# Packed keys for the second batch of a fused attention and gated feed-forward kernel, and weight units stored before their split

## The chip, the core and the metric

The kernel runs on one core of a Trainium2 chip. The metric is device time in microseconds (us), the median of several runs. On the core TensorE (PE in the profile) multiplies matrices, VectorE (DVE), ScalarE (ACT) and GpSimd (POOL) work element by element, and SyncE (SP) issues most transfers (DMA). Sums of TensorE go to PSUM, which has eight banks; an evacuation is the copy of a sum out of PSUM.

## The reference

Softcapped attention over 4 batches of 12 heads, 448 positions and 64 columns a head; its result, 1792 tokens of 768 columns, goes through a gated feed-forward layer.

```python
def _attn_ref(q, k, v, cap):
    scores = np.matmul(q, k.transpose(0, 1, 3, 2)) / np.sqrt(q.shape[-1])
    scores = cap * np.tanh(scores / cap)
    attn = np.exp(scores - np.max(scores, axis=-1, keepdims=True))
    attn = attn / (np.sum(attn, axis=-1, keepdims=True) + 1e-09)
    return np.matmul(attn, v).astype(np.float32)

x = attn_out.transpose(0, 2, 1, 3).reshape(B * S, H * D)
gate = 1.0 / (1.0 + np.exp(-(x @ w_gate)))     # x 1792x768, w_gate and w_val 768x1536
out = (gate * (x @ w_val)) @ w_out             # w_out 1536x768
```

The three weights arrive as 64-bit floats.

## The kernel before

**Precision.** Most products take each factor as two 32-bit parts of reduced precision, `hi` and `lo` (`_Ops.hi`, L207, a rounding copy; `_Ops.lo`, L213, the difference), and add three products. Products of probabilities and values are made in plain fp32 for the first twelve head pairs instead (`direct(n)`, n < 12); such a product shows as two matmul records a piece.

**Attention** (`_bounded_attention`) works on 24 pairs of heads, n = 0 to 23, six a batch. For each pair it transposes keys and queries (`emit_T`, tile `tp`), copies them out as hi and lo (tile `T`), makes scores in four groups of keys (`emit_S`, tile `sc`, a two-bank PSUM tile, head 0 in one bank and head 1 in the other; each matmul uses half of the rows of TensorE, "64*112" in its row), takes tanh out of PSUM into `t` (L392), takes exp once a head (`emit_exp`, L400), and multiplies with the values (`emit_PV`, tile `pv`). The values carry 64 columns of ones, so that `pv` holds the sums of exp too. `emit_rd` copies `pv` out (L479 the sums, L481 the values), a reciprocal and a product follow (L506, `emit_out`). For n < 6 (`packed`) keys stand in three groups of 128 and a last one that holds the last 64 keys of both heads: its scores are three matmuls over all rows (L379), its part of `pv` two fp32 matmuls with half the rows (`emit_R`, L434), and the other part three fp32 matmuls a head (L441). For n = 6 to 11 (`even`) keys stand in four groups of 112: 24 score matmuls (L389) and four fp32 matmuls a head (L450), issued two at a time, each head in the one bank of the pool `ps_v` after the other.

**Feed-forward** (`moe(b)`) takes 36 weight units a batch: 24 units of 18 matmuls into `h` (L836; gate unit, then value unit) and 12 units of 18 into `o` (L927). In batch 0 each unit u is loaded as 64-bit words, converted to fp32 in one of two raw slots of `pair0` (L728 on ACT, L729 to L731 on DVE, five units ahead of its use), split into `wspl` (L207 on ACT, L213 on DVE, three units ahead; four slots, `WB`), and the split unit, 768 KB, is stored to DRAM (L777, tile `wd`) to be loaded again in batches 1 to 3 (L787). Units 0 to 3 are split early and stored through ACT's queue (`next_w`).

**Order.** The attention of batch b+1 is woven into the feed-forward of batch b. `_emit` draws from both generators: a `yield` says how much work was issued, and attention goes on when `done_a * tot_m <= done_m * tot_a`, where `tot_m` is 545 and `tot_a` is 12 times `o.head(b + 1)`. PE and ACT run in exactly this order. DVE, POOL and SP are ordered by a list scheduler.

Of the kernel before, what the change touches and what calls it, by code (L numbers as in the profile page):

```python
# [98 lines left out]
def _load_inside(engines, t, src, n, runs=False):  # L99

    s = _pair(src, n)
    order = "(p c) d -> p c d" if runs else "(c p) d -> p c d"
    for h in range(2):
        engines[h % len(engines)].dma_start(
            out=t[0:src.shape[2] // NCH, :, h, :], in_=s[h].rearrange(order, c=NCH)
        )


def _load_evenly(nc, t, src, n):

    s = _pair(src, n)
    for h in range(2):
        nc.sync.dma_start(
            out=t[0:src.shape[2] // NCH, h * NCH:(h + 1) * NCH],
            in_=s[h].rearrange("(p c) d -> p c d", c=NCH),
        )
# [132 lines left out]
def _bounded_attention(o, x_done):  # L249
# [66 lines left out]
    def load_v(n):  # L316
# [8 lines left out]
        if packed(n):  # L325
            _load_v_packed(nc, s[:, :, 0:D], o.v, n)
        else:
            _load_evenly(nc, s[:, :, 0:D], o.v, n)
# [11 lines left out]
    def emit_T(n):  # L340
# [5 lines left out]
        if even(n):  # L346
            o.transpose_evenly(ps[:, 0, :], t[:, 1])
        else:
            for m in range(NC):
                nc.tensor.transpose(  # L350
                    ps[:, 0, m * P:(m + 1) * P], t[:, 1, m].rearrange("p h d -> p (h d)"), ident
                )
# [2 lines left out]
        w = S if even(n) else BANK
        hi, lo = T[n][:, 0, :, 0:w], T[n][:, 1, :, 0:w]
        if even(n):
            parts = [(hi, lo, ps[:, :, 0:w])]
        else:
            parts = [tuple(  # L360
                x.rearrange("p i s -> p (i s)")[:, 0:BANK + S] for x in (hi, lo, ps)
            )]
        for a, b, x in parts:
            o.hi("a", a, x)
            with o.tc.high_priority(offset=2 * AHEAD_OF):
                o.lo("v", b, x, a)
# [656 lines left out]
```

## Time and profile before

| | us |
| --- | --- |
| median of 3 runs (lowest to highest) | 760.43 (759.23 to 761.16) |
| profiled execution | 758.98 |
| its span on the core | 757.2 |
| PE busy | 742.8 (98%) |
| DVE busy | 467.4 (62%) |
| ACT busy | 349.4 (46%) |
| POOL busy | 202.3 (27%) |

The mean granted clock of TensorE was 0.999 of full speed. The core moved 170.63 MB; the transfers that SP issued took 69.8% of the time of the 16 DMA engines. Busy time says how long an engine had something to run; a row with a bracket names the idle time just before it and what ended that.

### The profile page before, as it was taken

How to read it: one execution, taken by the hardware profiler on the slowest of the kernel's cores; microseconds unless marked ns; L12 is line 12 of the kernel's file. 1: busy time of each engine (PE TensorE's matmuls, PEld its weight loads, DVE VectorE, ACT ScalarE, POOL GpSimd, SP SyncE). 2: the span in 40 equal slices, each digit the busy share in tenths (PEclk: the TensorE clock that was granted, in tenths of full speed). 3: DMA queues.
4: the chain of work that ended last, by engine and by line, in shares of the span. 5: the costliest groups of instructions: out<-in, count | busy, mean ns of one | idle time of the engine just before them, and what ended most of it. 6: DMA issues, size and time to landing. Idle time of an engine off the chain costs nothing.

```text
span 757.2 us, 10267 instructions
## 1 busy us (share of the span) xinstructions
PE 742.8 (98%) x3922; PEld 642.5 (85%) x3922; DVE 467.4 (62%) x503; ACT 349.4 (46%) x383; POOL 202.3 (27%) x223
## 2 busy tenths in 40 slices
PE   8999999999999999999999999999999999999997
PEld 7555878777778888988899988888889999999996
DVE  2698789979998938878786628878785011111000
ACT  5888577667576445555554245555540000000000
POOL 1354000021210516363535306353551000000000
PEclk9999999999999999999999999999999999999999
DMA  4867899999999866555677956644589866665541
GB/s 100 222 161 156 284 346 360 330 307 302 285 267 376 298 212 196 179 186 178 183 222 232 288 185 193 199 143 158 166 234 313 273 223 226 226 225 180 176 168 56
DMA packets 133509, 170.63 MB, mean 225 GB/s; under 512 B 86860, under 2 KB 111948, under 8 KB 133452
## 3 DMA queue, kind: packets, MB, share of 16 engines
q1 hardware_dynamic: 131788, 166.44, 69.8%
q10 hardware_dynamic: 1664, 3.46, 1.3%
q8 instruction: 33, 0.54, 0.3%
q14 instruction: 24, 0.20, 0.1%
HBM read 132.91 MB, written 36.18 MB: 223 GB/s over the span
## 4 chain that ended last, share of the span: by engine, by line
PE 78%; DVE 10%; DMA 3%; SPq 2%; issue 2%; POOL 2%; ACT 2%; DVEq 0%; POOLq 0%; ACTq 0%
PE h L836 43%; PE o L927 18%; PE sc L389 5%; PE pv L450 4%; DVE rd L506 2%; PE pv L459 2%; PE pv L460 2%; DVE pl L213 1%; PE tp L242 1%; DMA v<-in_v_dram 1%; PE pv L441 1%; DVE pair L731 1%; PE tp L350 1%; DVE pair L730 1%; DVE wspl L213 1%
## 5 line engine op out<-in xcount | busy, mean ns | idle before, releaser
L836 PE MATMUL h<-xspl,wspl 128*128 128x448 f32 x1728 | 377.4, 372 | 0.3 <-DVE osb L949 0.3
L836 PEld LDWEIGHTS h<-xspl,wspl 128*128 128x128 f32 x1728 | 321.3, 188 | 42.4 <-issue 15.5
L927 PE MATMUL o<-wspl,gspl 128*128 128x384 f32 x864 | 159.3, 338 | 0.2 <-DVE osb L949 0.2
L927 PEld LDWEIGHTS o<-wspl,gspl 128*128 128x128 f32 x864 | 150.5, 188 | 4.8 <-issue 3.8
L392 ACT ACTIVATE t<-sc,scale 128x896 f32<-128x896 f32 (+1 forms) x90 | 85.9, 1002 | 43.9 <-PE sc L389 43.7
L205 POOL TENSOR_SCALAR gspl<-gate 128x448 fp32r<-128x448 f32 x48 | 35.9, 748 | 251.7 <-DVE gate L880 251.7
L877 ACT ACTIVATE gate<-h 128x448 f32<-128x448 f32 x48 | 26.0, 541 | 161.3 <-PE h L836 159.8
L400 ACT ACTIVATE t<-t,capv 128x1792 f32<-128x1792 f32 (+2 forms) x48 | 83.2, 1738 | 0.1
L880 DVE SCALAR_TENSOR_TENSOR gate<-gate,h 128x448 f32<-128x448 f32 x48 | 29.7, 618 | 77.1 <-PE h L836 72.1
L506 DVE RECIPROCAL rd<-rd 128x448 f32<-128x448 f32 x24 | 70.7, 2946 | 5.3 <-ACT rd L479 3.1
L389 PE MATMUL sc<-T 64*128 64x448 f32 (+1 forms) x540 | 69.1, 382 | 1.9 <-DVE T L213 1.7
L389 PEld LDWEIGHTS sc<-T 64*128 64x128 f32 (+1 forms) x540 | 46.4, 181 | 22.3 <-issue 10.9
L949 DVE TENSOR_SCALAR osb<-o 128x384 f32<-128x384 f32 x22 | 12.0, 553 | 73.1 <-PE o L927 73.0
L412 POOL TENSOR_TENSOR a<-t 128x448 f32<-128x448 f32 x24 | 31.6, 1315 | 84.8 <-ACT t L400 46.9
L213 DVE TENSOR_TENSOR gspl<-gate,gspl 128x448 fp32r<-128x448 f32 x48 | 36.6, 763 | 22.3 <-POOL gspl L205 22.1
L207 ACT ACTIVATE ph<-t 128x1792 fp32r<-128x1792 f32 x24 | 40.7, 1696 | 16.4 <-PE pv L461 10.1
L213 DVE TENSOR_TENSOR pl<-t,ph 128x1344 fp32r<-128x1344 f32 x24 | 45.6, 1899 | 2.4 <-ACT ph L207 1.9
L213 DVE TENSOR_TENSOR T<-tp,T 128x960 fp32r<-128x960 f32 (+1 forms) x24 | 27.3, 1136 | 27.8 <-ACT T L207 27.8
L731 DVE SCALAR_TENSOR_TENSOR pair<-w,pair 128x768 uint16<-128x768 uint32 x36 | 41.7, 1162 | 0.3
L728 ACT ACTIVATE pair<-w 128x768 f32<-128x768 f32 x36 | 32.5, 904 | 18.9 <-DVE wspl L213 7.2
L450 PE MATMUL pv<-t,vo 112*128 112x448 f32 x96 | 40.1, 539 | 0.4 <-ACT t L400 0.4
L730 DVE SCALAR_TENSOR_TENSOR pair<-w,pair 128x768 int32<-128x768 int32 x36 | 35.5, 990 | 0.6
(81 smaller groups left out, 716.3 us busy)
## 6 DMA issues: line engine op xcount, KB each, us to landing
wspl<-wd SPq DMA_DIRECT2D x108, 768.0 KB, 4.4
wd<-wspl SPq DMA_DIRECT2D x32, 768.0 KB, 6.3
w<-in_moe_w_gate_dram SPq DMA_DIRECT2D x12, 768.0 KB, 6.7
w<-in_moe_w_val_dram SPq DMA_DIRECT2D x12, 768.0 KB, 7.0
w<-in_moe_w_out_dram SPq DMA_DIRECT2D x12, 768.0 KB, 7.1
qk<-in_q_dram SPq DMA_DIRECT2D x46, 112.0 KB, 4.1
out_dram<-osb SPq DMA_DIRECT2D x24, 192.0 KB, 3.3
qk<-in_k_dram SPq DMA_DIRECT2D x34, 96.0 KB, 2.7
```

Of the source, the lines that this page charges most:

```text
L205: self.nc.gpsimd.tensor_scalar(dst, src, 1.0, 1.0, ALU.mult, ALU.mult)
L207: self.nc.scalar.activation(dst, src, AF.Copy)
L213: e.tensor_sub(dst, src, hi.bitcast(F32))
L389: nc.tensor.matmul(ps[0:w, j, 0:S], a[rows], r[rows], start=(i == 0), stop=(i == len(ops) - 1))
L392: nc.scalar.activation(Pt[n][0:w, :, m, :], ps[0:w, :, 0:S], AF.Tanh, scale=c["scale"][0:w])
L400: nc.scalar.activation(t, t, AF.Exp, scale=c["cap"][rows])
L450: nc.tensor.matmul(pv, vs[n][0:QC, j * NC + m, :], Pt[n][0:QC, j, m, :], start=(m == 0), stop=(m == NC - 1),)
L506: nc.vector.reciprocal(rd, rd)
L730: nc.vector.scalar_tensor_tensor(xi, top, -2 ** 31, xi, ALU.bitwise_and, ALU.bitwise_or)
L731: nc.vector.scalar_tensor_tensor(half, low.bitcast(U32), 2.0 ** -29, half, ALU.mult, ALU.add)
L836: nc.tensor.matmul(ps, a, r, start=(kk == 0 and i == 0), stop=(kk == KD - 1 and i == 2))
L927: nc.tensor.matmul(ps, a, r, start=(y + kk == 0 and i == 0), stop=(y + kk == KF - 1 and i == 2),)
```

## The change

Three things change. First, `packed` becomes `direct`, so pairs 6 to 11 use the packed form of pairs 0 to 5. For these pairs (`together(n)`) both heads' `pv` stand in one two-bank tile from the pool of the scores, and the last score group of pairs 7 to 11 stands in the bank of `ps_v` that is free by it. The main loop has a new branch for the step after such a pair: the two half-row matmuls, the first score group, both heads' products, four copies out of `pv`, the other three score groups, the transposes, both exps. Second, `o.head` is 23.5 where it was 25, and 17.8 for the last batch; at n = 24 two yields of 5 are added. Third, odd units 5 to 27 (`whole`) are stored once converted, before their split, 384 KB each (tile `wr`), loaded again to a raw slot seven units ahead in batches 1 to 3, and split again there: 12 more splits a batch on ACT and DVE, no split store for these units.

```diff
-    packed = alone
+    packed = direct
+    def together(n):
+        return direct(n) and not alone(n)
...
-    o.head = lambda b: 25 if direct(b * o.NPAIR) else 18.5
+    o.head = lambda b: 23.5 if direct(b * o.NPAIR) else 17.8 if b == B - 1 else 18.5
...
+        if packed(n) and m == NF:
+            if together(n) and n > o.NPAIR:
+                ps = o.ps_v.tile([P, S], F32, tag="v", name=f"sc{n}_{m}")
+            else:
+                ps = o.two_banks(f"sc{n}_{m}")[:, 0, 0:S]
+            for i, (a, r) in enumerate(ops):
+                nc.tensor.matmul(ps, a, r, start=(i == 0), stop=(i == len(ops) - 1))
+            nc.scalar.activation(Pt[n][:, 0, NF, :], ps, AF.Tanh, scale=c["scale"])
+            return 4
...
+    two = {}
     def new_pv(n, j):
-        if alone(n) and not (j == 1 and n % 2 == 0):
+        if together(n):
+            if j == 0:
+                two[n] = o.two_banks(f"pv{n}")
+            pv = two[n][:, j, 0:S] if j == 0 else two.pop(n)[:, j, 0:S]
+        elif alone(n) and not (j == 1 and n % 2 == 0):
...
+        if n > 0 and together(n - 1):
+            emit_R(n - 1)
+            emit_S(n, 0)
+            yield 5
+            for j in range(2):
+                for _ in emit_PV(n - 1, j):
+                    yield 6
+            for j in range(2):
+                emit_rd(n - 1, j)
+            emit_out(n - 1)
+            vs.pop(n - 1)
+            load_v(n + 1)
+            yield 5
+            emit_S(n, 1)
+            emit_S(n, 2)
+            if not packed(n):
+                yield 8
+            emit_S(n, NF)
+            yield 8
+            emit_T(n + 1)
+            qks[n + 2] = o.load_qk(n + 2, packed(n + 2))
+            yield 5
+            if n % o.NPAIR == 0:
+                yield None
+            emit_exp(n, 0)
+            if not direct(n):
+                emit_P(n, 0)
+            emit_exp(n, 1)
+            split_v(n + 1)
+            if direct(n):
+                yield 15
+            continue
...
+        if not live:
+            yield 5
...
+        if not live:
+            yield 5
...
+    WHOLE = 28
...
+    def whole(u):
+        u %= NU
+        return u % 2 == 1 and KEEP <= u < WHOLE and o.early == KEEP
...
         w_raw[u] = x
+        if whole(u):
+            d = dram.tile([P, UN], F32, name=f"wr{u}")
+            w_dram[u] = d
+            nc.sync.dma_start(out=d, in_=x)
...
-        if not u < KEEP:
+        if KEEP <= u < NU and not whole(u):
             store_w(u, s)
...
+    def load_raw_to(n):
+        while loaded["raw"] < min(n, B * NU):
+            u = loaded["raw"]
+            loaded["raw"] += 1
+            if NU <= u and whole(u):
+                at = loaded["slot"] % WRAW * UN
+                loaded["slot"] += 1
+                x = c["pair0"][:, at:at + UN]
+                nc.sync.dma_start(out=x, in_=w_dram[u % NU])
+                w_raw[u] = x
...
-            if KEEP <= u < o.early or NU <= u:
+            if KEEP <= u < o.early or NU <= u and not whole(u):
...
         load_to(u + WB)
+        load_raw_to(u + LEAD + 2)
```

In the rows that follow a tile has its name and numbers (`pv6`, `h0_0_1` is batch, which, chunk; `wspl5` the split unit 5), and lines of the changed kernel have moved: L836 is L865 there, L927 is L956, L434 L413, L441 L420, L389 L365, L728 L741, L207 L197, L479 and L481 are L449 and L451.

PE where batch 0's feed-forward begins, before: the third unit's matmuls, the scores of pair 7, then the first products of pair 6 with its values.

```order
L836 MATMUL h0_0_1_812<-xspl0_4_655,wspl2_521 128x448 x3
L389 MATMUL sc7_0_835<-T7_725 112x448 x6
L389 MATMUL sc7_1_843<-T7_725 112x448 x6
L836 MATMUL h0_0_1_812<-xspl0_5_697,wspl2_521 128x448 x3
L836 MATMUL h0_1_1_868<-xspl0_0_319,wspl3_603 128x448 x3
L836 MATMUL h0_1_1_868<-xspl0_1_405,wspl3_603 128x448 x3
L836 MATMUL h0_1_1_868<-xspl0_2_491,wspl3_603 128x448 x3
L836 MATMUL h0_1_1_868<-xspl0_3_573,wspl3_603 128x448 x3
L450 MATMUL pv6_0_881<-t6_663,vo6_658 128x448 x2
```

The same place on PE after: the half-row products of pair 6 are the first instruction after the third unit.

```order
L865 MATMUL h0_0_1_822<-xspl0_4_663,wspl2_521 128x448 x3
L865 MATMUL h0_0_1_822<-xspl0_5_706,wspl2_521 128x448 x3
L413 MATMUL pv6_848<-t6_672,vo6_666 128x448 x2
L365 MATMUL sc7_0_852<-T7_731 128x448 x6
L865 MATMUL h0_1_1_876<-xspl0_0_319,wspl3_607 128x448 x3
L865 MATMUL h0_1_1_876<-xspl0_1_405,wspl3_607 128x448 x3
```

The products of pair 6 now stand after 54 matmuls of `h`, ahead of the scores of pair 7; they stood after 66 and 12 score matmuls of pair 7.

ACT around the end of unit 18 of batch 0, before: the gate of `h0_0_9`, the conversion of unit 23, the split of unit 22, the copies out of pair 9's first head, the tanh of pair 10's later score groups.

```order
L877 ACTIVATE gate0_9_1568<-h0_0_9_1580 128x448
L728 ACTIVATE pair0_66<-w64_23_1477 128x768
L207 ACTIVATE wspl22_1608<-pair0_66 128x768
L479 ACTIVATE rd9_1620<-pv9_0_1562 64x448
L481 ACTIVATE xraw1_928<-pv9_0_1562 64x448
L392 ACTIVATE t10_1533<-sc10_2_1623,scale_94 112x2x448
L392 ACTIVATE t10_1533<-sc10_3_1631,scale_94 112x2x448
```

The same place on ACT after:

```order
L906 ACTIVATE gate0_9_1579<-h0_0_9_1589 128x448
L741 ACTIVATE pair0_66<-w64_23_1502 128x768
L197 ACTIVATE wspl22_1620<-pair0_66 128x768
L449 ACTIVATE rd9_1632<-pv9_1555 64x448
L451 ACTIVATE xraw1_929<-pv9_1555 64x448
L449 ACTIVATE rd9_1632<-pv9_1555 64x448
L451 ACTIVATE xraw1_929<-pv9_1555 64x448
L368 ACTIVATE t10_1558<-sc10_1_1650,scale_94 128x2x448
L368 ACTIVATE t10_1558<-sc10_2_1658,scale_94 128x2x448
```

All four copies of pair 9 stand in a row behind gate, conversion and split, and ahead of the tanh of pair 10's second score group.

PE after, around it: from the last products of pair 9 to the scores of pair 10 that take the bank pair of `pv9` again.

```order
L420 MATMUL pv9_1555<-t9_1321,vo9_1172 128x448 x3
L865 MATMUL h0_0_9_1589<-xspl0_4_663,wspl18_1449 128x448 x3
L865 MATMUL h0_0_9_1589<-xspl0_5_706,wspl18_1449 128x448 x3
L865 MATMUL h0_1_9_1625<-xspl0_0_319,wspl19_1504 128x448 x3
L865 MATMUL h0_1_9_1625<-xspl0_1_405,wspl19_1504 128x448 x3
L865 MATMUL h0_1_9_1625<-xspl0_2_491,wspl19_1504 128x448 x3
L865 MATMUL h0_1_9_1625<-xspl0_3_577,wspl19_1504 128x448 x3
L365 MATMUL sc10_1_1650<-T10_1476 128x448 x6
L365 MATMUL sc10_2_1658<-T10_1476 128x448 x6
L358 MATMUL sc10_3_1666<-T10_1476 128x448 x3
```

Between the last product of pair 9 and group 2 of pair 10 stand 18 matmuls of `h` and one score group.

PE at the end of attention, in the feed-forward of batch 2, before: from the last product of pair 23's first head to the first of its second head.

```order
L461 MATMUL pv23_0_5053<-ph23_0_4992,vs23_4831 128x448
L927 MATMUL o2_0_2_4982<-wspl97_4897,gspl2_3903 128x384 x6
L927 MATMUL o2_0_0_4980<-wspl98_4951,gspl2_3903 128x384 x6
L927 MATMUL o2_0_1_4981<-wspl98_4951,gspl2_3903 128x384 x6
L459 MATMUL pv23_1_5097<-pl23_1_5085,vs23_4831 128x448
```

The same place on PE after:

```order
L431 MATMUL pv23_0_5147<-ph23_0_5066,vs23_4894 128x448
L956 MATMUL o2_0_2_5035<-wspl99_5036,gspl2_3934 128x384 x6
L956 MATMUL o2_0_0_5033<-wspl100_5057,gspl2_3934 128x384 x6
L956 MATMUL o2_0_1_5034<-wspl100_5057,gspl2_3934 128x384 x6
L956 MATMUL o2_0_2_5035<-wspl100_5057,gspl2_3934 128x384 x6
L956 MATMUL o2_0_0_5033<-wspl101_5099,gspl2_3934 128x384 x6
L956 MATMUL o2_0_1_5034<-wspl101_5099,gspl2_3934 128x384 x6
L429 MATMUL pv23_1_5211<-pl23_1_5179,vs23_4894 128x448
```

The second head of pair 23 stands 36 matmuls of `o` behind the first, where 18 stood. Ahead of the first head there are 24 between it and the row sums of pair 22 (`dn22`), where there were 6.

## Rows read from the trace of the kernel before

**Rows 1.** The page: busy time, share of the span and instructions of each engine.
```profile
PE 742.8 (98%) x3922; PEld 642.5 (85%) x3922; DVE 467.4 (62%) x503; ACT 349.4 (46%) x383; POOL 202.3 (27%) x223
```

**Rows 2.** Chain of waits: start us, length us, engine, output tile, line, count.
```profile
113.47 1.41 PE sc L389 x12
...
117.50 1.51 PE pv L450 x4
119.00 2.44 PE h L836 x12
...
570.40 3.12 PE o L927 x18
```

**Rows 3.** Timeline of PE, 24 to 36: start, length, line, tile, shape, count [idle before].
```profile
26.61 0.92 PE L434 MATMUL pv<-t,vo 64*128 64x448 f32 x4
27.46 2.52 PE L441 MATMUL pv<-t,vo 128*128 128x448 f32 x6
...
32.20 2.43 PE L441 MATMUL pv<-t,vo 128*128 128x448 f32 x6
34.56 0.47 PE L389 MATMUL sc<-T 64*128 64x448 f32 x2
```

**Rows 4.** Timeline of PE, 535 to 605, the end of attention.
```profile
562.40 0.44 PE L459 MATMUL pv<-pl,vs 128*128 128x448 f32 x1 [0.99 <-DVE xraw L488]
...
568.69 0.47 PE L459 MATMUL pv<-pl,vs 128*128 128x448 f32 x1 [1.48 <-DVE pl L213]
```

**Rows 5.** Timeline of PE: start of batch 0's feed-forward, and tile tp of pair 12.
```profile
73.71 0.99 PE L242 MATMUL tp<-ident,qk 112*128 112x112 f32 x8 [0.49 <-ACT t L392]
74.47 10.58 PE L836 MATMUL h<-xspl,wspl 128*128 128x448 f32 x51
...
90.14 1.77 PE L450 MATMUL pv<-t,vo 112*128 112x448 f32 x4 [0.44 <-ACT t L400]
...
214.57 0.66 PE L350 MATMUL tp<-ident,qk 128*128 128x128 f32 x4 [0.90 <-ACT t L392]
```

**Rows 6.** Timeline of ACT, 60 to 92.
```profile
87.56 0.85 ACT L207 ACTIVATE wspl<-pair 128x768 fp32r<-128x768 f32 x1 [2.72 <-PE h L836]
...
88.31 3.45 ACT L400 ACTIVATE t<-t,capv 112x1792 f32<-112x1792 f32 x2
```

**Rows 7.** Chain of waits, 80 to 92: the store of split unit 1.
```profile
82.07 5.41 DMA wd<-wspl
```

**Rows 8.** Timeline of ACT, 130 to 200: gate, conversion of unit 23, copies of pair 9.
```profile
179.69 0.55 ACT L877 ACTIVATE gate<-h 128x448 f32<-128x448 f32 x1 [3.41 <-PE h L836]
180.13 0.90 ACT L728 ACTIVATE pair<-w 128x768 f32<-128x768 f32 x1
...
182.34 0.54 ACT L481 ACTIVATE xraw<-pv 64x448 f32<-64x448 f32 x1
```

**Rows 9.** Timeline of ACT, 100 to 130: the conversion of unit 11.
```profile
111.97 0.91 ACT L728 ACTIVATE pair<-w 128x768 f32<-128x768 f32 x1
```

**Rows 10.** Timeline of DVE: last conversion step of units 9 and 21.
```profile
107.97 1.06 DVE L731 SCALAR_TENSOR_TENSOR pair<-w,pair 128x768 uint16<-128x768 uint32 x1
...
174.32 1.01 DVE L731 SCALAR_TENSOR_TENSOR pair<-w,pair 128x768 uint16<-128x768 uint32 x1
```

**Rows 11.** Stores of split units (768 KB) from issue to landing, 100 to 200.
```profile
DMA to landing us min/median/max: 3.6/6.2/8.3
```

**Rows 12.** The page's DMA issues: KB each, us to landing.
```profile
out_dram<-osb SPq DMA_DIRECT2D x24, 192.0 KB, 3.3
```

**Rows 13.** Timeline of PE: first and warm 128x128 matmuls, and the last matmuls.
```profile
1.64 3.78 PE L72 MATMUL warm<-ident 128*128 128x128 f32 x16 [1.64 <-POOL ident masks.py:199]
...
13.80 1.96 PE L304 MATMUL fill<-ident 128*128 128x128 f32 x16
...
745.22 6.40 PE L927 MATMUL o<-wspl,rest 128*128 128x384 f32 x36
```

**Rows 14.** Windows after the last matmul: length, engines' busy time, granted clock.
```profile
756.20:756.40 0.20, 0.00 (x0) 0.00 (x0) 0.00 (x0) 0.00 (x0) 0.00 (x0) 0.87 0.00 0
```

More of the change, by code (lines that the diff above doesn't have):

```diff
@@ L96, in _pair, with _load_inside @@
     return src[b, 2 * p:2 * p + 2]
-def _load_inside(engines, t, src, n, runs=False):
+def _load_inside(engines, t, src, n):
     s = _pair(src, n)
-    order = "(p c) d -> p c d" if runs else "(c p) d -> p c d"
     for h in range(2):
         engines[h % len(engines)].dma_start(
[L105 to L115, printed above, removed]
+            out=t[0:src.shape[2] // NCH, :, h, :],
+            in_=s[h].rearrange("(c p) d -> p c d", c=NCH),
         )
@@ L324, in load_v @@
         nc.gpsimd.memset(s[:, :, D:], 1.0)
[L325 to L328, printed above, removed]
+        _load_v_packed(nc, s[:, :, 0:D], o.v, n)
         vs[n] = s
@@ L345, in emit_T @@
         ps = o.two_banks(f"tp{n}")
[L346 to L352, printed above, removed]
+        for m in range(NC):
+            nc.tensor.transpose(
+                ps[:, 0, m * P:(m + 1) * P], t[:, 1, m].rearrange("p h d -> p (h d)"), ident
+            )
         o.transpose_evenly(ps[:, 1, :], t[:, 0])
         T[n] = ap.tile([P, 2, 2, BANK], F32R, tag="T", bufs=1, name=f"T{n}")
[L355 to L366, printed above, removed]
+        a, b, x = (
+            y.rearrange("p i s -> p (i s)")[:, 0:BANK + S]
+            for y in (T[n][:, 0], T[n][:, 1], ps)
+        )
+        o.hi("a", a, x)
+        with o.tc.high_priority(offset=2 * AHEAD_OF):
+            o.lo("v", b, x, a)
     def emit_S(n, m):
@@ L371, in emit_S @@
             Pt[n] = ap.tile([P, 2, NC, S], F32, tag="t", bufs=2, name=f"t{n}")
-        w = QC if even(n) else P
-        kh, kl = (T[n][:, i, 0, m * w:(m + 1) * w] for i in range(2))
+        kh, kl = (T[n][:, i, 0, m * P:(m + 1) * P] for i in range(2))
         qh, ql = (T[n][:, i, 1, 0:S] for i in range(2))
         ops = ((kh, qh), (kl, qh), (kh, ql))
-        ps = o.two_banks(f"sc{n}_{m}")
-        if packed(n) and m == NF:
-            for i, (a, r) in enumerate(ops):
-                nc.tensor.matmul(
-                    ps[:, 0, 0:S], a, r, start=(i == 0), stop=(i == len(ops) - 1)
-                )
-            nc.scalar.activation(
-                Pt[n][:, 0, NF, :], ps[:, 0, 0:S], AF.Tanh, scale=c["scale"]
-            )
-            return 4
+        if packed(n) and m == NF:
[7 more added lines that the diff above has]
+            return 4
+        ps = o.two_banks(f"sc{n}_{m}")
         for i, (a, r) in enumerate(ops):
@@ L389, in emit_S @@
                 nc.tensor.matmul(
-                    ps[0:w, j, 0:S], a[rows], r[rows], start=(i == 0), stop=(i == len(ops) - 1)
+                    ps[:, j, 0:S], a[rows], r[rows], start=(i == 0), stop=(i == len(ops) - 1)
                 )
-        nc.scalar.activation(
-            Pt[n][0:w, :, m, :], ps[0:w, :, 0:S], AF.Tanh, scale=c["scale"][0:w]
-        )
+        nc.scalar.activation(Pt[n][:, :, m, :], ps[:, :, 0:S], AF.Tanh, scale=c["scale"])
         return 4
     def emit_exp(n, j):
-        rows = slice(0, QC if even(n) else P)
-        t = Pt[n][rows, j, 0:NF if packed(n) and j == 1 else NC]
-        nc.scalar.activation(t, t, AF.Exp, scale=c["cap"][rows])
+        t = Pt[n][:, j, 0:NF if packed(n) and j == 1 else NC]
+        nc.scalar.activation(t, t, AF.Exp, scale=c["cap"])
     def emit_P(n, j):
@@ L777, in store_w @@
         queue.dma_start(out=d.bitcast(F32), in_=s.bitcast(F32))
-    loaded = {"next": 0}
+    loaded = {"next": 0, "raw": 0, "slot": 0}
+    def load_raw_to(n):
[8 more added lines that the diff above has]
+                w_raw[u] = x
     def load_to(n):
```

33 lines of the change are left out of this document (10 added, 23 removed).

## The prediction

> **What bounds the kernel now.** I read the busy shares first: PE is busy for 742.8 of 757.2 us and the next engine, DVE, for 467.4 [rows 1]. The chain of waits agrees: wherever the feed-forward runs it is PE after PE, scores, products with values and `h` in turn [rows 2]. So an edit is worth what it takes from PE's own matmuls, plus the idle brackets on PE's timeline that it removes, less those that it makes. The brackets at stake are few: 0.49, 0.44 and 0.90 around batch 0 [rows 5], 0.99 and 1.48 at the end of attention [rows 4]. Work on DVE, ACT or a queue counts only where PE comes to wait for it. The sum is made against the profiled execution, 758.98 (span 757.2 and 1.8 around it); the same difference is then put to the median, 760.43, which lies 1.45 above it.
>
> **Part 1, the packed form on PE.** For one pair of the second batch the old form has two score runs of 12 half-row matmuls, 1.41 each, and four runs of two fp32 products, 1.50 each [rows 2]. Three key groups of 128 keep 18 of the 24 score matmuls, so half a run goes, 0.70, and all four product runs, 6.00. What comes: three score matmuls over all rows, at the rate of `h` (2.44 for 12) 0.61 [rows 2]; the two half-row products, 0.85 from 26.61 to 27.46; and two runs of three fp32 products [rows 3]. Such a run took 2.36, from 32.20 to 34.56 [rows 3]; at the rate of the old runs (0.75 a product) it would be 2.25. Two runs are 4.50 to 4.72, and I take 4.61. A pair changes by -6.70 + 0.61 + 0.85 + 4.61 = -0.63, six pairs by **-3.8** (-4.4 to -3.1). Transposes cost the same number of matmuls; nothing hides this term, since PE does it itself.
>
> **Part 2, the end of attention.** Pair 23's first head waits 0.99 for a copy on DVE and its second 1.48 for the low part of its probabilities [rows 4]. The smaller head values and the two added yields put 24 matmuls of `o` where 6 stood ahead of the first, and 36 where 18 stood ahead of the second. Eighteen take 3.12 [rows 2], more than either wait, and they are only moved from behind. So both waits go: **-2.5**. DVE may come later by 2.1 at the first head and 1.6 at the second before a wait returns; if it uses that up, the term is 0.
>
> **Part 3, pair 12.** Its transposes wait 0.90 for a tanh on ACT [rows 5]. By the new order 18 matmuls of `o` stand between the last scores of pair 11 and these transposes: **-0.9** (0 if ACT is late there).
>
> **Part 4, the first products of pair 6.** Here the change makes a wait. PE comes to `h` at 74.47, after an idle 0.49 that ended with a tanh, and takes 51 matmuls in 10.58, some 0.205 each [rows 5]. The old order put 66 of them and 12 score matmuls ahead of the products of pair 6, which still waited 0.44 for the exp, to 90.14 [rows 5]. The new order has 54 ahead and nothing else. What the exp waits for is not moved: on ACT it stands behind the split of unit 5, which started at 87.56 when the slot of unit 1 was free, that is when the store of unit 1, issued at 82.07, had landed 5.41 later [rows 6, 7]. The split takes 0.85 and the first of the two exps (3.45 together) half of 3.45 [rows 6], so PE gets it at 90.1 again. It arrives at 74.47 - 0.49 + 54 x 0.2035 (2.44 for 12 [rows 2]) = 84.97, and waits 5.1. Behind the waiting instruction stands all of PE; everyone waits with it. Removed are 0.49 and 0.44, so the net is **+4.2**. If the store landed in 3.6, the least of its kind [rows 11], it would be +2.4; in 8.3, the most, +7.1. I take 5.41, the duration of this very store.
>
> **Part 5, evacuation.** Both heads of a pair now share a two-bank tile, and the third score group of the next pair takes it again, so it waits for the fourth copy. The old form gave `pv` a bank of its own. The order shows pair 9: PE needs 18 `h` (3.66) and a score run of 6 (0.70) from the last product to that group, 4.36. ACT first waits for the end of unit 18, 6 `h` or 1.22 after the last product, then does gate, conversion, split and one head's two copies, 2.65 up to the start of the second [rows 8], and that copy and two more, 0.56 each: 1.22 + 2.65 + 3 x 0.56 = 5.55. Wait: **+1.2**. At pair 7 the same count gives about 0, elsewhere ACT does no conversion between and is ahead. Bounds 0 (ACT early by its idle time) and 4 (three places like it).
>
> **Part 6, unsplit units.** In batches 1 to 3 twelve units each are split again: a copy on ACT, 0.85 [rows 6], and a subtraction on DVE, of which the trace gives the nearest of the same width as 1.01 [rows 10]. That is some 10 us of ACT and 12 of DVE a batch, spread over 180 us of PE, three units ahead of use; DVE is free for 290 us in all [rows 1]. SP's raw loads wait for the subtraction that frees the slot, with the other loads queued behind; a unit of 18 `h` is 3.66, so three units are 11 us of cover. I take +0.3 (0 to +2). In batch 0 the store of a raw unit reads its slot, so the conversion two units later, on ACT, must wait for its landing. Unit 9 ended its conversion at 109.03 and unit 11 began at 111.97, 2.9 later; unit 21 ended at 175.33 and unit 23 began at 180.13, 4.8 later [rows 8, 9, 10]. How long 384 KB take the trace doesn't show: 192 KB took 3.3 and 768 KB 6.2 [rows 11, 12]. In proportion between them I take 4.3, with 0.3 for the issue 4.6: unit 11 late by 1.7, unit 23 by nothing. ACT passes on perhaps half: +0.8 (0 to +5.3, below). The smaller traffic takes nothing from PE, which waits for no weights now: 0.
>
> **Sum:** -3.8 - 2.5 - 0.9 + 4.2 + 1.2 + 0.3 + 0.8 = -0.7. That makes 758.3 for an execution like the profiled one and **759.7** against the median. The gain on PE is real and one new wait eats most of it.
>
> **Rivals.** *The wait is short (faster).* If the store of unit 1 lands in 3.6, the new wait loses 1.8; if ACT reaches pair 9's copies early and the raw stores land in time, 1.2 and 0.8 go too: -0.7 - 3.8 = -4.5, or 755.9. For it: the landing varies from 3.6 to 8.3 [rows 11], and ACT idles often just ahead of these places (3.41 ahead of the gate [rows 8]). Against it: the store met the same traffic before, and it took 5.41 [rows 7].
>
> *ACT held by raw stores (slower).* ACT runs in order. A conversion that waits for the landing of its slot's store holds the split, copies, tanh and exp behind it, and PE waits for the bank pair that the copies free. If a raw store takes 6.2, like a whole split unit, then with 0.3 for issue unit 11 is late by 6.5 - 2.9 = 3.6 and unit 23 by 6.5 - 4.8 = 1.7, the latter right ahead of pair 9's copies, where there is nothing to spare. All of it on PE is 5.3 in place of my 0.8: 759.7 + 4.5 = **764.2**. It decides from a landing of some 4.5 us at unit 23. For it: DMA is densest in batch 0. Against: half the bytes, and fewer of them in all.
>
> *The clock falls in the new wait.* After the last matmul, which ended at 745.22 + 6.40 = 751.62, the granted clock still averaged 0.87 in the slice from 756.20 [rows 13, 14]: PE had been idle for some 4.7 us when it fell. A wait of 5.1 us is at that edge. The first 16 matmuls of the kernel, at the lower level of 1.2 GHz, took 3.78, and the same 16 warm, at 2.4 GHz, took 1.96 [rows 13]: 1.8 lost, hence 761.5. The Trainium skill says in "TensorE: Matmul & The Clock Gate", section "HAM oscillation — how this bites in real kernels", that idle gaps between bursts of matmuls lower TensorE's clock, so that the work after a gap is slow too; by that rule the new wait costs more than its length. The idle end of this trace agrees that a gap of that size is enough, and no gap inside the run is long enough to test it.
>
> *The order does not do what it says.* The waits of part 2 stay because DVE, with the added subtractions, is late by the same amount: +2.5, or 762.2. The slack of 1.6 to 2.1 stands against it.
>
> **How the numbers follow.** A measurement of this kernel can tell about 0.3%, 2.3 us, from no change: faster is below 758.1, slower above 762.7. Forecast, 0.46: its own range 757.3 to 762.0 by parts 1, 4 and 5, with 0.05 of it faster. Short wait, 0.28, all but 0.01 faster. ACT held, 0.16, slower. Clock, 0.07, with 0.03 slower (if the low level lasts longer than at the start). Waits of part 2 stay, 0.03, within. That is 0.32 faster, 0.49 within, 0.19 slower. The range takes in the short wait with the low end of part 1 (755.3) and the most likely form of ACT held: 755.3 to 764.3.
>
> **What the changed profile would show.** Part 1: runs of `pv` and scores that total about 6.1 a pair. Part 4: the largest idle bracket on PE, about 5 us at 85 to 90, released by the exp of ACT, with the split of unit 5 and the landing of unit 1's store ahead of it in the chain; a bracket under 3 or over 6.5 proves the term wrong. Part 5: a bracket of about 1.2 on a score group of pair 10, released by a copy on ACT. Parts 2 and 3: no bracket at pairs 23 and 12. Part 6: no PE bracket that ends with a split on DVE; a bracket on ACT at a conversion that ends with a raw store's landing is the slower rival. A lower granted clock just after 90 is the clock rival. If PE shows none of these waits and still no gain, the sum of part 1 is wrong.

## Result: slower by 1%

The changed kernel takes 766.59 us (765.70 to 768.30, four runs) where the kernel before took 760.07 beside it: a ratio of 1.0099 (1.0084 to 1.0113), +6.5 us. Forecast were 759.7 and a range of 755.3 to 764.3; the time lies outside it, on the slow side. The profiled execution took 767.25 (span 765.5) against 758.98, +8.3. The page after, engines as in [rows 1]:

```profile
PE 743.0 (97%) x3904; PEld 643.5 (84%) x3904; DVE 502.7 (66%) x539; ACT 374.8 (49%) x419; POOL 213.6 (28%) x235
```

PE has fewer instructions and the same busy time. The timeline of PE shows the waits of over 1 us after 80 us, and a row behind the first:

```profile
91.13 1.86 PE L413 MATMUL pv<-t,vo 64*128 64x448 f32 x4 [4.84 <-ACT t L373]
...
94.04 4.17 PE L865 MATMUL h<-xspl,wspl 128*128 128x448 f32 x12
...
191.37 0.88 PE L365 MATMUL sc<-T 64*128 64x448 f32 x6 [1.22 <-ACT xraw L451]
...
234.13 1.86 PE L413 MATMUL pv<-t,vo 64*128 64x448 f32 x4 [2.49 <-issue]
...
253.94 2.37 PE L956 MATMUL o<-wspl,gspl 128*128 128x384 f32 x12 [1.49 <-DVE osb L978]
...
566.96 2.35 PE L956 MATMUL o<-wspl,gspl 128*128 128x384 f32 x12 [1.22 <-DVE gate L909]
```

The wait at pair 6 is there, 4.84 where 0.44 stood [rows 5]. Behind it twelve `h` take 4.17; twelve took 2.44 [rows 2]. The windows tell why (stretch, length, busy time of PE, PEld, DVE, ACT, POOL, granted clock, DMA share, GB/s):

```profile
88.00:90.00 2.00, 0.00 (x0) 0.00 (x0) 1.48 (x2) 1.45 (x2) 0.00 (x0) 1.00 1.07 402
90.00:91.00 1.00, 0.00 (x0) 0.00 (x0) 0.39 (x1) 1.00 (x2) 0.00 (x0) 0.73 1.05 372
91.00:92.00 1.00, 0.87 (x2) 0.51 (x4) 0.00 (x0) 1.00 (x2) 0.00 (x0) 0.50 1.10 364
96.00:97.00 1.00, 1.00 (x4) 0.87 (x4) 0.56 (x1) 0.59 (x2) 0.00 (x0) 0.50 1.09 383
97.00:98.00 1.00, 1.00 (x6) 0.92 (x5) 0.99 (x2) 0.64 (x1) 0.00 (x0) 0.85 1.17 379
```

The granted clock falls to 0.50 (1.2 GHz) late in the wait and is back at full (2.4 GHz) from 98. The same happens behind the wait at 234, with 0.50 from 234 to 237. ACT, where the exp of pair 6 stands behind a split that waits for a store:

```profile
88.55 0.84 ACT L197 ACTIVATE wspl<-pair 128x768 fp32r<-128x768 f32 x1 [2.76 <-DMA wd<-wspl]
...
89.30 3.08 ACT L373 ACTIVATE t<-t,capv 128x1792 f32<-128x1792 f32 x2
```

Stages of the feed-forward, each from its first `h` or `o` on PE's timeline to the first of the next stage, in us. `h` and `o` of batch 1 and `h` of batch 2 are left out: 121.0 to 121.2, 48.2 to 48.3 and 120.2 to 120.3 in all these kernels; so are `h` and `o` of batch 3, 89.3 and 62.6. The pace moves attention work between the two stages of batch 0, so kernels are compared by the sum.

| kernel | batch 0 h | batch 0 o | sum | batch 2 o | median |
| --- | --- | --- | --- | --- | --- |
| before | 133.3 | 56.7 | 190.0 | 45.6 | 760.07 |
| after | 141.2 | 58.2 | 199.4 | 44.1 | 766.59 |
| pair 6's exps early (e1) | 134.4 | 59.1 | 193.6 | 44.2 | 761.46 |
| before, new tail (f3) | 133.2 | 57.1 | 190.3 | 42.9 | 757.21 |
| e1, head 22 (i4) | 128.4 | 57.9 | 186.3 | 44.2 | 754.29 |
| e1, head 22, all split stored (k2) | 128.4 | 58.6 | 187.0 | 43.4 | 753.61 |

All of the loss is in batch 0. Its o stage holds less attention work than before (one pair's products with values, where one and a half stood), and is longer all the same. The idle brackets on PE in both stages sum to 1.5 before, 10.5 after and 2.4 in i4.

### The profile page after: what moved, and what is told of

It is laid out like the page before. It is cut to its first block, busy times and chain, and to the rows that moved or that the text cites. A ratio compares the mean times of both kernels' runs of the same rounds, so it can differ in the third digit from the quotient of the medians.

```text
span 765.5 us, 10391 instructions
## 1 busy us (share of the span) xinstructions
PE 743.0 (97%) x3904; PEld 643.5 (84%) x3904; DVE 502.7 (66%) x539; ACT 374.8 (49%) x419; POOL 213.6 (28%) x235
## 4 chain that ended last, share of the span: by engine, by line
PE 80%; DVE 9%; DMA 4%; SPq 2%; issue 2%; ACT 2%; POOL 1%; ACTq 0%; DVEq 0%; POOLq 0%
PE h L865 43%; PE o L956 20%; PE sc L365 5%; PE pv L420 4%; DVE rd L476 2%; PE pv L430 2%; PE pv L429 2%; DMA w<-in_moe_w_out_dram 1%; DVE pair L743 1%; DMA v<-in_v_dram 1%; DVE pair L744 1%; PE pv L413 1%; PE tp L332 1%; PE tp L230 1%; DVE wspl L203 1%
## 5 line engine op out<-in xcount | busy, mean ns | idle before, releaser
L865 PE MATMUL h<-xspl,wspl 128*128 128x448 f32 x1728 | 374.3, 371 | 0.2 <-DVE xspl L203 0.2
L865 PEld LDWEIGHTS h<-xspl,wspl 128*128 128x128 f32 x1728 | 322.7, 189 | 38.6 <-issue 10.8
L956 PE MATMUL o<-wspl,gspl 128*128 128x384 f32 x864 | 158.0, 337 | 3.0 <-DVE osb L978 1.8
L956 PEld LDWEIGHTS o<-wspl,gspl 128*128 128x128 f32 x864 | 150.2, 188 | 7.0 <-issue 2.5
L197 ACT ACTIVATE wspl<-pair 128x768 fp32r<-128x768 f32 x68 | 57.4, 844 | 91.8 <-PE h L865 70.4
L368 ACT ACTIVATE t<-sc,scale 128x896 f32<-128x896 f32 x84 | 80.8, 1004 | 31.0 <-PE sc L365 30.5
L373 ACT ACTIVATE t<-t,capv 128x1792 f32<-128x1792 f32 (+1 forms) x48 | 80.4, 1688 | 0.0
L203 DVE TENSOR_TENSOR wspl<-pair,wspl 128x768 fp32r<-128x768 f32 x68 | 73.3, 1078 | 4.1 <-ACT wspl L197 4.0
L365 PE MATMUL sc<-T 64*128 64x448 f32 x504 | 69.6, 399 | 3.1 <-DVE T L203 1.7
L365 PEld LDWEIGHTS sc<-T 64*128 64x128 f32 x504 | 45.0, 188 | 24.6 <-issue 13.8
L420 PE MATMUL pv<-t,vo 128*128 128x448 f32 x144 | 58.6, 544 | 0.0
L197 ACT ACTIVATE ph<-t 128x1792 fp32r<-128x1792 f32 x24 | 40.8, 1698 | 14.5 <-PE pv L431 14.4
L420 PEld LDWEIGHTS pv<-t,vo 128*128 128x128 f32 x144 | 26.4, 189 | 22.5 <-issue 21.5
L203 DVE TENSOR_TENSOR T<-tp,T 128x960 fp32r<-128x960 f32 x24 | 27.6, 1149 | 22.8 <-ACT T L197 22.8
```

Of the source, the lines that this page charges most:

```text
L197: self.nc.scalar.activation(dst, src, AF.Copy)
L203: e.tensor_sub(dst, src, hi.bitcast(F32))
L365: nc.tensor.matmul(ps[:, j, 0:S], a[rows], r[rows], start=(i == 0), stop=(i == len(ops) - 1))
L368: nc.scalar.activation(Pt[n][:, :, m, :], ps[:, :, 0:S], AF.Tanh, scale=c["scale"])
L373: nc.scalar.activation(t, t, AF.Exp, scale=c["cap"])
L420: nc.tensor.matmul(pvs[n, j], vs[n][:, j * NC + m, :], Pt[n][:, j, m, :], start=False, stop=(m == NF - 1),)
```

## Experiments

Beside them the kernel before stood at 759.3 to 759.7. A ratio is to the kernel before, with its 95% interval. In these kernels the lines lie up to six further down (L867 or L869 for L865, L958 for L956).

### The wait at pair 6 and the clock behind it

e1_exp6_early:

```diff
-                done_a, tot_a = 30, tot_a + 30
+                done_a, tot_a = 3, tot_a + 30
...
         emit_exp(n, 1)
         split_v(n + 1)
+        if first:
+            yield 27
```

> The changed kernel with one thing moved: the two exps of pair 6 are issued after 6 matmuls of h instead of after 54, so that on ACT they stand ahead of the split of unit 4 and of the split of unit 5, which waits for the store of unit 1. PE's order stays: the half-row products of pair 6 still follow the 54 matmuls of h. Theory 1 (the exp behind the store makes the wait of 4.84 us, and that idle time drops the clock, 0.50 granted from 91 to 97, which costs some 3 us more): both go, about 766.6 - 7.8 = 758.8, and no slice near 90 has a granted clock under 1.00. Rival (PE is held at this place by the unit stores themselves, whatever stands behind them): the wait comes back within the next three units, at the matmuls of unit 5 or at the scores of pair 7, and the time stays at 764 to 767.

761.46 us: 5.1 less than the changed kernel. The wait and the low clock at 90 are gone and do not come back within three units; the h stage falls from 141.2 to 134.4. But 761.5 is not 758.8: the o stage still waits 5.07, and a wait of 1.16 at a score group of pair 7, behind the copies of pair 6 and hidden before behind the late PE, is new.

e3_fill_wait (`fill2` is a tile in the bank of `ps_v`):

```diff
         if n > 0 and together(n - 1):
+            if n - 1 == o.NPAIR:
+                for _ in range(36):
+                    nc.tensor.matmul(fill2, ident, ident, start=True, stop=True)
             emit_R(n - 1)
```

> The changed kernel with 36 matmuls of 128x128 into an unused bank put ahead of the half-row products of pair 6; their result is not used. They take some 0.12 us each when the clock is full, 4.4 in all, and so fill the wait of 4.84 without ending it: the products still start near 91.1. Theory 1 (the idle time lowers the clock): the granted clock stays 1.00 from 90 to 98, the matmuls behind the products run at full rate, and the time falls by some 3 us to 763.6. Rival (the low clock is not from the idle time but from what runs there, half-row fp32 products with dense DMA): the clock is low at 91 to 97 as before and the time is 766 to 767.

769.43 us. The filler was mis-sized: 36 such instructions are 72 records, 8.2 us, and ended 3 us too late. The timeline of PE:

```profile
85.94 8.20 PE L502 MATMUL fill<-ident 128*128 128x128 f32 x72
94.07 1.02 PE L413 MATMUL pv<-t,vo 64*128 64x448 f32 x4
...
95.63 2.70 PE L869 MATMUL h<-xspl,wspl 128*128 128x448 f32 x12
```

It still tells the theories apart. The granted clock stayed at 1.00 from 85 to 99, twelve `h` behind took 2.70 in place of 4.17, with the same products and a DMA share as high (0.98 to 1.23 between 90 and 94). From the products of pair 6 to the third score group of pair 10 it is 97.41 here (94.07 to 191.48) and 100.24 in the changed kernel (91.13 to 191.37): the low clock cost 2.8.

k1_only_head_22 (`o.head` at 22 in place of 23.5, exps of pair 6 as in the change):

> The changed kernel (766.6) with the head value of batch 1 at 22 in place of 23.5, and nothing else: the exps of pair 6 stay behind the store of unit 1. If the two faults are separate, the wait of 4.8 at pair 6 and its low clock stay and the idle time of the o stage goes: 754.3 + 5.1 (what the early exps gave) + up to 2 = 759.4 to 761.4. Rival (one fault: the o stage's idle time is the echo of the wait at pair 6 or the other way round): near 754 or near 766.

768.49 us, slower than the change. The slower weave puts pair 6 six `h` later, behind the next unit's start, so that its exps stand behind one more split on ACT, which waits for one more store:

```profile
88.27 0.84 ACT L197 ACTIVATE wspl<-pair 128x768 fp32r<-128x768 f32 x1 [2.60 <-DMA wd<-wspl]
...
96.51 0.84 ACT L197 ACTIVATE wspl<-pair 128x768 fp32r<-128x768 f32 x1 [5.11 <-DMA wd<-wspl]
...
97.26 3.08 ACT L373 ACTIVATE t<-t,capv 128x1792 f32<-128x1792 f32 x2
```

PE waits 11.73 there, and in the o stage only 1.20. The forecast time, 759.4 to 761.4, missed by 7 because of the first number. The second says that there are two faults, each with its own place.

### Second splits, and the tail

e4_all_split_stored (`WHOLE = 0`):

> The changed kernel without its third part: every unit from 4 on is stored split and loaded split again (no raw stores, no second split). Theory 1 (waits on PE at pairs 6, 10 and 11 come from the order on ACT; the units add only the DVE waits of batches 1 and 2): the wait at pair 6 and its clock stay, the wait of 1.22 for the gate on DVE at 567 and part of the waits of 1.75 for o's evacuation at 248 to 254 go, 766.6 - 1 to 2.5 = 764 to 765.5. Rival (the raw stores and the added DVE work are what makes the change slow): waits at pairs 10 and 11 go too, and with their clock: 759 to 761.

764.72 us, 1.9 less, with 1.0072 (1.0053 to 1.0090) against 1.0099 (1.0084 to 1.0113): the intervals overlap a little. The wait of 1.22 at 567 went, and with it 1.2 of the tail; those at pairs 6, 10 and 11 stayed (4.82, 1.22, 2.49). So what this part of the change costs in the tail is shown; the rest is not, since the low clock was shorter behind pair 6 in this trace and did not come behind pair 11.

f3_before_tail_only (the kernel before, `o.head` at 17.8 for the last batch, two `yield 5`):

> The kernel before with only the second part of the change for the last batch: the head value of 17.8 and the two yields of 5 at the last step. The prediction said that the two waits at pair 23, 0.99 and 1.48, then go: 759.6 - 2.5 = 757.1. In the changed kernel one wait of 1.22 for the gate on VectorE stood in this stage, and it was not there without the second splits (e4_all_split_stored). Rival (that wait comes from the new order by itself): 758.3 with a wait of 1.2 near 565.

757.21 us, 0.9967 (0.9957 to 0.9977) of the kernel before: 2.3 gained, both waits of [rows 4] gone and none in their place.

### The o stage of batch 0

ACT in the changed kernel there; the last row is the exps of pair 11, of which the first ends at 234.0. PE starts at 234.13; its bracket names no releaser ("issue"), and e2 shows that these exps are what it waits for:

```profile
223.65 0.94 ACT L741 ACTIVATE pair<-w 128x768 f32<-128x768 f32 x1 [2.01 <-DVE wspl L203]
227.97 0.85 ACT L197 ACTIVATE wspl<-pair 128x768 fp32r<-128x768 f32 x1 [3.39 <-DVE pair L744]
...
230.71 0.92 ACT L741 ACTIVATE pair<-w 128x768 f32<-128x768 f32 x1 [1.03 <-DVE wspl L203]
...
232.26 3.08 ACT L373 ACTIVATE t<-t,capv 128x1792 f32<-128x1792 f32 x2
```

e2_exp11_early (the changed kernel, the two `emit_exp` of n = 11 right after `emit_S(n, NF)`):

> The changed kernel with one thing moved: the two exps of pair 11 are issued right after its last tanh, ahead of the conversion of unit 29, the splits of units 28 and 29, the conversion of unit 30 and the copy of tile T of pair 12, which in the changed kernel all stand ahead of them on ACT and wait 2.0, 3.4 and 1.0 us for DVE. Theory 1 (ACT, in order, passes DVE's backlog of 212 to 235 us on to the exp): the wait of 2.49 us at the half-row products of pair 11 goes, with the low clock of 234 to 237 behind it, some 1.6 us: 766.6 - 4.1 = 762.5. Rival (DVE's backlog reaches PE by another way, the splits, which come 3 us later now): a wait of 2 to 3 us at the o matmuls of units 28 to 31, and the time stays within 1 us of 766.6.

766.57 us, nothing gained. The wait at pair 11 went, and 2.95 at the evacuation of `o`, where 1.49 stood, and 1.18 at a score group of pair 12 came: the rival. The idle time of the stage is 4.13 where it was 4.24.

f1_lo_on_pool (e1, with `o.lo("p" ...)` for units 24 to 35):

> The kernel with pair 6's exps early (e1_exp6_early, 761.46), and the low parts of units 24 to 35 of batch 0 made on GpSimd in place of VectorE: 12 subtractions of some 1.0 us leave VectorE there, and cost GpSimd, which is idle for most of that stage, 1.8 each. Where exp of pair 11 was moved early, its wait went and a wait of 2.95 for the evacuation of o and one of 1.18 for tanh came in its place. Theory 2 (VectorE's queue is the second bound of batch 0's o stage, so whatever is moved on ACT, its lateness comes back at another place): the idle time of 5.07 in that stage falls to 1 or 2, and the low clock there with it: 761.46 - 3 to 4.5 = 757 to 758.5. Rival (the loads of the 64-bit weights, which ACT waited 4.2 for there, are the bound): idle time in that stage stays at 4 to 5 and the time at 761.

763.23 us, no gain: 1.0042 (1.0025 to 1.0059), where e1 has 1.0026 (1.0011 to 1.0041). Idle time in the stage rose from 5.07 to 7.04. A low part takes 1.8 to 2.5 on GpSimd and 0.95 on DVE, and ACT's conversions now wait for GpSimd (1.84 and 1.66): the chain of a unit became longer. f6_before_lo_on_pool, the same edit in the kernel before:

> The kernel before with the low parts of units 24 to 35 of batch 0 made on GpSimd in place of VectorE, the control of f1_lo_on_pool. The kernel before has idle brackets of 0.90, 0.16 and 0.32 in that stage. Theory 2 (VectorE's queue bounds the stage only when PE's own work has become shorter): at most 1.4 is gained, 758.2 to 759.6. Rival (VectorE bounds the stage in either kernel beyond what the brackets show): 756 to 757.

760.46 us, 1.0016 (1.0006 to 1.0026): nothing gained there either.

g4_loads_on_pool_queue (e1, `load_w64` on `nc.gpsimd` for u >= 31) and h4_tail_and_loads (f3 with the same):

> The kernel with pair 6's exps early (e1_exp6_early, 761.46), and the loads of the 64-bit weights of units 31 to 35 issued by GpSimd in place of SyncE. Theory 3 (in batch 0's o stage SyncE's queue stands still at stores of split units that wait for their low part on VectorE; the load of unit 33 stands behind two of them, so ACT waits for it, 4.2 us, then VectorE's conversion, then the evacuation of o that stands behind it on VectorE, then PE): ACT's waits for weight loads in 225 to 245 go, the wait of 2.56 at the evacuation of o falls to 0.5 or less, and the time to 758.5 to 759.5; the wait at pair 11's first products, 2.51, which comes before, stays. Rival (the transfers are slow because the DMA engines are full there, not because of their place in the queue): the same waits, 761 to 762.

> The kernel before with the new tail (f3_before_tail_only, 757.2), and the loads of units 31 to 35 issued by GpSimd: the control of g4_loads_on_pool_queue. In this kernel's o stage of batch 0 the brackets on PE sum to 1.53. Theory 3: SyncE's queue held loads there too (ACT waited 1.5, 2.3 and 1.2 for them), so up to 1 is gained: 756.2 to 757.2. Rival (place in the queue doesn't matter): 757.2.

760.27 and 757.24 us. In g4 the single wait of 2.56 at the evacuation of `o` became two of 1.35 and 1.50, and the idle time of the stage 5.92; the low clock of 240 to 250 went with the longer gap. The loads went out no earlier from GpSimd's queue (221.5 to 238.1 us, against 222.1 to 237.0 in e1), and ACT still waited 5.8 for them, against 6.5. In h4 ACT's waits for them fell from 8.7 to 1.6, and the time did not move. So in h4's kernel these waits cost nothing, and in e1 what holds the loads is not shown.

i1_short_reciprocal (e1, `nc.vector.reciprocal` over `rd[:, 0:8]` for n = 10 and 11):

> The kernel with pair 6's exps early (e1_exp6_early, 761.46), with the reciprocals of pairs 10 and 11 taken over 8 of 448 columns only; this leaves out part of the computation, 2 x some 2.8 us of VectorE. Theory 4 (the reciprocal of pair 10, 2.94, lands in VectorE's conversion of units 27 and 28, and that of pair 11 between the evacuations of o; ACT and PE wait for what stands behind them): the waits of 2.51 at pair 11 and 2.56 at the evacuation of o fall under 1 each, the low clock there goes, the o stage falls from 59.1 to 55 or 56 and the time to 757 to 758. Rival (the stage is held by the loop of load, conversion and split itself): 760 to 761.5, idle time over 3.5.

760.15 us (757.42 to 761.59). The wait at pair 11 went, one of 3.30 at the evacuation of `o` stayed, and the stage is 57.0 long, not 55 or 56. The reciprocals are a cause of the first wait, and of 2 of the stage's length in this trace; by the time, 1.0002 (0.9986 to 1.0018), the gain over e1 isn't resolved.

i3_head_25 and i4_head_22 (e1, `o.head` of batch 1 at 25 and at 22):

> The kernel with pair 6's exps early (761.46), with the head value of batch 1 at 25 again, where the change has 23.5: attention is woven in faster, so that pair 11's first products stand after unit 25 of batch 0 in place of unit 27, and its scores ahead of the o stage. Theory 5 (the pace puts pair 11's exps behind conversions that VectorE serves late): the wait at pair 11 goes and the evacuation of o comes free of the second reciprocal: 757 to 758.5. Rival (the stage has the same conversion work in any weave): idle time in the h stage grows by what the o stage loses, 760 to 762.

> The kernel with pair 6's exps early (761.46), with the head value of batch 1 at 22, the other way: pair 11's first products stand after unit 29. Theory 5 (pace): pair 11 meets the conversion of units 32 to 34 and the change of o's accumulators, idle time of 4 to 6 stays, 761 to 763. Rival (more matmuls ahead of pair 11 give ACT the time that it lacks): the wait of 2.51 goes, 758 to 759.

761.41 and **754.29 us**. At 25 the wait at pair 11 went and came back as 4.53 at pair 7, with the clock at 0.50 behind it; there ACT's copies stand behind a split that waits for the store of a unit:

```profile
101.12 0.84 ACT L197 ACTIVATE wspl<-pair 128x768 fp32r<-128x768 f32 x1 [3.53 <-DMA wd<-wspl]
101.99 0.54 ACT L449 ACTIVATE rd<-pv 64x448 f32<-64x448 f32 x1
```

At 22 PE's timeline has two brackets of over 1 us left between 80 and 550:

```profile
160.49 0.87 PE L365 MATMUL sc<-T 64*128 64x448 f32 x6 [1.23 <-ACT xraw L451]
...
233.78 1.33 PE L958 MATMUL o<-wspl,gspl 128*128 128x384 f32 x6 [1.19 <-DVE osb L980]
```

The rival of i4 held in its sign, against the theory on record: the wait at pair 11 went. The time is 4 under the rival's, and its reason, more matmuls ahead of pair 11 that give ACT time, is not what the traces show (below). The mean granted clock is 0.998 there.

### The shared bank pair

f2_copies_by_head (e1, `emit_rd(n - 1, j)` inside the loop over heads):

> The kernel with pair 6's exps early (761.46), and the copies of pv issued head by head: those of head 0 follow its products, ahead of head 1's, where all four stood behind both. Theory (the wait of the third score group of pairs 8 and 10, 1.16 and 1.23, is for the fourth copy, which stands behind gate, conversion and split on ACT): two copies, 1.1, are done earlier, so both waits fall to about 0.1 and the time by 2.2 to 759.3. Rival (in that place ACT's gate and conversion set the time, and head 1's copies wait all the same): under 0.5 is gained.

763.32 us (761.10 to 765.41), no gain. The first of the two waits is at a score group of pair 7, not 8: it follows the products and copies of pair 6. Both waits went, but both heads are one tile, and the products of head 1 now wait for the copies of head 0:

```profile
95.96 4.05 PE L420 MATMUL pv<-t,vo 128*128 128x448 f32 x6 [2.91 <-ACT xraw L451]
```

h5_bank_group_first (e1, for pairs 7 to 11 `emit_S(n, NF)` ahead of `emit_S(n, 2)`):

> The kernel with pair 6's exps early (761.46), and for pairs 7 to 11 the last score group, which goes to the free bank of ps_v, made ahead of the third, which waits for the fourth copy out of the two-bank tile. Theory (the waits of 1.16 and 1.23 at pairs 8 and 10 are a matter of a microsecond of order): the three full matmuls, 0.80, now run in the wait, so both waits fall to about 0.4 and the time by 1.6 to 759.9. Rival (the tanh of the moved group stands ahead of the others on ACT and delays the transposes or exps): no gain, 761 to 762, with a wait at a later group.

761.61 us. Both waits (at pairs 7 and 10) fell as expected, to 0.37 and 0.42, and the h stage by 0.2 alone (134.2). The moved group lies between two half-row groups, and the trace shows that this order costs PE time: at pair 9, which waits in neither kernel, the three groups take 2.43 where they took 2.13 in e1. From the first products of one pair to those of the next, pairs 7 and 10 gain 0.31 and 0.46, and pairs 8 and 9 lose 0.16 and 0.46.

### Together

h3_several_mended (e1, `WHOLE = 0`, g4's loads, h5's order):

> The changed kernel with four of its waits mended together: pair 6's exps early, all units stored split (no second split), the loads of units 31 to 35 issued by GpSimd, and the bank group ahead of the third score group. By the single runs: 766.6 - 5.1 (exps) - 1.9 (no raw stores) - 2 (loads) - 1.6 (bank group) = 756.0; PE's own work is 3.8 less than before and the tail 2.3 less, so with no wait left but that at pair 11, 2.5, it would be 759.5 - 3.8 - 2.3 + 2.5 - 0.9 = 755.0. Rival (batch 0 is bound by its weight conversion, so that every wait mended comes back behind it in the o stage): 758 to 760, no better than the kernel before with the tail alone (757.2).

759.12 us, 0.9993 (0.9984 to 1.0003): the rival. The o stage still waits 4.21.

j2_split_head_25 (e1, `WHOLE = 0`, head 25):

> Pair 6's exps early, all units stored split, head 25: the packed form and the new tail with the wait at pair 6 mended and the old pace. If theory 5 holds: the time of i3_head_25 less 1.2 for the tail's wait, 755.5 to 757.3, faster than the kernel before with the new tail alone (757.2). If it doesn't: 759 to 760.5.

761.68 us, with 5.17 at pair 7: theory 5 has the wrong sign.

k2_split_head_22 (e1, `WHOLE = 0`, head 22):

> Pair 6's exps early, head 22, and all units stored split, as in the kernel before. The tail's wait of 1.24 for the gate on VectorE goes, as in the three kernels without second splits: 754.3 - 1.2 = 753.1. Rival (the raw stores relieve the DMA of batch 0 and are worth as much there): 754 to 755.5.

**753.61 us, 0.9926 (0.9910 to 0.9943)** of the kernel before, and 13 under the change. The tail's wait went (43.4 against 44.2); i4 with raw stores has 0.9927 (0.9905 to 0.9949), so the gain of storing all units split isn't resolved.

## Why the prediction was wrong, step by step

Two steps failed: part 4 priced the wait at pair 6 by its length and left out the low clock behind it (2.8), and no part of the sum had the waits that the change makes in the o stage of batch 0 (2.9 of idle time and 1.4 of low clock).

- **Part 1 was right.** The chain of waits after has 0.95 for the half-row products, 0.61 + 1.42 + 0.80 for the scores, 2.25 for each run of three products: 8.28 a pair, where the old form has 8.86 by [rows 2]. Six pairs change by -3.5:

```profile
162.38 1.42 PE sc L365 x12
163.80 0.80 PE sc L358 x3
...
175.78 0.95 PE pv L413 x4
176.73 0.61 PE sc L365 x6
...
178.75 2.25 PE pv L420 x6
```

With PE's clock full, in i4 and k2, PE is busy 738.7 where it was 742.8: -4.1. The forecast, -3.8, lies between the two. The busy time of the change itself, 743.0, holds matmuls at half clock.
- **Parts 2 and 3** were right in mechanism: the waits of [rows 4] and the 0.90 of [rows 5] went. Part 2 gained 1.2 in place of 2.5, since a gate on DVE comes late by 1.22 in every kernel here that has second splits in its tail and in none that stores all units split (e4, h3, j2, k2); without them it is 2.3 (f3). The prediction gave +0.3 for all second splits.
- **Part 4** named the wait, its cause and its size: 4.84 against 5.1. It failed in its price. I counted the length of the idle time and put the clock at a chance of 0.07 and a price of 1.8; the low clock cost another 2.8 (e3), so the term was 6.7 and not 4.2. The Trainium skill, "TensorE: Matmul & The Clock Gate", section "HAM oscillation — how this bites in real kernels", says that idle gaps between matmuls lower the clock; the trace agrees here, with 0.50 behind 4.84 of idle time. The row at the end of the trace [rows 14] had said as much, and should have moved the forecast.
- **Part 5** was right: 1.22 at pair 10, forecast 1.2. That no other pair waits was wrong once PE comes on time: 1.16 at pair 7, behind the copies of pair 6, in e1.
- **Part 6**: raw stores landed in 5.5 to 6.8, median 6.1, where I took 4.3; ACT waited 2.7 for them in all, and no PE bracket ends there. The slower rival by that mechanism did not occur, although its time, 764.2, is near the result.
- **The step that was missing** is the o stage of batch 0. The prediction read the order at pair 6, pair 9 and pair 23, and at pair 12 for its transposes, but not at the first products of pair 11, where ACT's exps stand behind three conversions and splits: idle time in the stage 4.2 in place of 1.4, and the clock at 0.50 from 234 to 237, 1.4 more (from the first products of pair 11 to the twelve `o` behind its first head PE takes 6.07, and 4.64 in e4, where the clock stayed at 1.00).

For the profiled execution: -4.1 (part 1) + 3.9 and 2.8 (pair 6 and its clock) + 1.2 (pair 10) + 2.9 and 1.4 (o stage and its clock) - 1.2 (tail) = +6.9 of the 8.3. Of the 1.4 left a longer wait for the values at 37 us is 0.6; the rest isn't placed.

**What was settled, what not.** The two faults are separate: moving the exps alone gives 5.1 (e1), head 22 alone loses 1.9 (k1), both give 12.3 (i4). Both are work that PE needs on an in-order ACT queue behind a split or conversion that waits for something far from attention: a store's landing, or DVE. Of the single mends in the o stage, e2 and i1 shifted the wait to the next evacuation, and f1 and g4 left it at pair 11.

Why head 22 frees the o stage was not tested by itself; the traces show this much. PE has 60 matmuls of `o` between the last scores of pair 11 and its first products in e1 and in i4 alike, so ACT gets no more time there. In e1 the reciprocal of pair 10 (2.95 on DVE, from 212.13) follows right behind the last gate of `h` (211.60), and the split ahead of pair 11's exps waits 3.41 for DVE. In i4 that reciprocal starts 10 us after the gate (217.53 and 207.52), and the split waits for PE alone:

```profile
225.32 0.85 ACT L197 ACTIVATE wspl<-pair 128x768 fp32r<-128x768 f32 x1 [2.59 <-PE o L958]
```

The later wait of e1, 2.56 at the evacuation of `o`, stands on DVE too. The evacuation comes behind conversion steps, these behind a conversion on ACT, and that behind its load; ACT waits for no such load there in i4. Rows of e1, ACT and then DVE:

```profile
238.56 0.90 ACT L743 ACTIVATE pair<-w 128x768 f32<-128x768 f32 x1 [4.23 <-DMA w<-in_moe_w_out_dram]
...
239.49 0.56 DVE L744 TENSOR_SCALAR pair<-pair 128x768 int32<-128x768 int32 x1 [2.50 <-ACT pair L743]
...
241.44 0.55 DVE L980 TENSOR_SCALAR osb<-o 128x384 f32<-128x384 f32 x1
```

An evacuation put ahead of these steps, or on another engine, was not tried.

## What to carry to other kernels

A shorter instruction stream on the bound engine meets its helpers earlier, so a change of form needs its own pace: here the same change is 1% slower at one pace and 0.7% faster at another, with the two exps of pair 6 moved (0.3% of that is the new tail alone, f3). Follow each first use on the bound engine back through the helper's in-order queue, and read what stands ahead of it, not what it needs. Price a wait of some microseconds on TensorE with the clock behind it, which cost more than half of the wait again where it fell (2.8 behind 4.84, 1.4 behind 2.49).

## What was not expected of the hardware

The granted clock of PE did not always fall at gaps of the same length. At 2.49 us idle it fell in the changed kernel (0.50 at 234 to 236) and not in e4 (1.00 from 230 to 240). At 2.65 in g4 it did not; at 2.73 in e3 it did (0.83 over 230 to 240). After 4.84, 4.53 and 11.73 it was at 0.50 each time. Nor was the low level always as long: behind pair 6 it held from 91 to 97 in the changed kernel, and in e4, after 4.82 of idle time, it was at 0.68 over 91 to 92, 0.50 to 94 and 1.00 from 95; the h stage is 1.1 shorter there. The runs of the changed kernel have mean clocks of 0.992 to 0.997 and lie 2.6 us apart; that this is the same effect is not shown.
